# v by a transposing load, paired scores, re-laid first keys and a new order for the first eight tiles, in a fused attention and feed-forward kernel

## The chip, the cores and the metric

The kernel runs on one core of one Trainium2 chip. The metric is the time of one execution in device microseconds. TensorE is called PE here, VectorE DVE, ScalarE ACT, GpSimd POOL and SyncE SP, as in the profile; PEld is PE's loading of weights.

## The reference

```python
kv_pool = kv.reshape(B, H // r, r, W // r, r, C).mean(axis=(2, 4))   # r = 4
k = v = kv_pool.reshape(B, -1, C) @ w_sr                  # 4 x 768 x 128
s = (1 / sqrt(C)) * (q @ k.transpose(0, 2, 1))            # q: 4 x 12288 x 128
s = s - s.max(-1, keepdims=True)
a = exp(s)
a /= a.sum(-1, keepdims=True) + 1e-09
x = a @ v
x_prev = x shifted by one row along the sequence, zero at the start
xk = mu_k * x + (1 - mu_k) * x_prev
xr = mu_r * x + (1 - mu_r) * x_prev
k = maximum(xk @ w_k, 0)                                  # w_k: 128 x 1024
out = sigmoid(xr @ w_r) * ((k * k) @ w_v)                 # w_v: 1024 x 128
```

All inputs and the output are float32. `mu_r` and `w_r` are scaled up by 64 in the inputs, `mu_k` and `q` by 8.

## The kernel before

There are four batches of 24 tiles, 96 tiles of T = 512 rows of q. A tile has four sub-tiles of 128 rows. Products that must be more exact than one 16-bit pass are sums of three passes over a high and a low part of each operand.

**A tile.** `qf` is loaded, ACT rounds it to `qh`, POOL takes the rest `ql`. For each sub-tile s, `S{s}` writes 128 x 768 scores into PSUM: in chunks of 512 and 256 columns first the corrections `ql` x `ksb` and `qb` x `ksl`, both 16-bit, then `qh` x `ksh` in float32r, which the profile shows as f32. DVE takes the row maximum (`nm`), ACT the exponential (`ex`, tile `pe`) with its sum, DVE the reciprocal (`rc`), ACT the high half of the probabilities (`f1`) and DVE the low half (`f2`), both in tile `pp`. A transposing load on SP (`tt`, `pT`<-`pp`) turns them. `AV0` to `AV5` multiply `pT` with the rows of v, `v1` high and `v2` low, into `px`; ACT and DVE make `xk` and `xr` from it; POOL the low parts. `ha`/`hb` make the hidden layer (`ph`, four pieces f of 256 columns of w_k), `r`, `k2`, `kh`, `kl` square it and split it, `va`/`vb` multiply with w_v into `pv`, `z` is the gate.

**Keys and v of a batch.** For batch 0 `first_keys` loads the 16 members of each pooling window (`L_a`, `L_b`: pieces of 512 and 256 columns, from `kv0`) and PE adds them up through `wsr` in float32 (`pk`). For a later batch DVE sums twelve blocks of windows (`br`, `acc`<-`kvt`, one per tile from tile SUM_AT on), and PE multiplies the sum (`pk0`, `pk1`). ACT scales it to `ks`. `ksh`, `ksl` and `ksb` are its parts for the scores. For v, DVE scales `ks` (`ksv`), PE transposes it in six 128 x 128 pieces (`pt0`, `pt1`), and ACT and DVE take its high and low half out of PSUM. `dg` is a diagonal matrix that PE multiplies with ones to spread per-channel maxima over all partitions; it shares `pt1`'s PSUM tile, and `xt` reads the result. PSUM tile `x` exists once, for `px`, `pz`, `pk`, `pt` and `cs`; the large `big` tiles for `S` and `ph` exist three times.

**The weights** w_k, w_v, w_r come as float64 bit patterns and are taken apart by DVE, ACT and POOL (`we` to `wo`), with one matmul `cs` per part.

**Order.** Every step is a function in a heap, sorted by a number, and each engine runs its instructions in just that order. `ONCE` has the numbers of the once-only steps, `EARLY` those of the first eight tiles, `WHEN` those of all others (plus i x PERIOD, 19.3), `LATE` those of the last four, `PREP` those of a later batch's preparation (from PREP_AT tiles on). All DMAs are issued by SP, in the same order, and an issue can wait until an earlier DMA has landed or a buffer is free.

Of the kernel before, what the change touches and what calls it, by code (L numbers as in the profile page):

```python
# [11 lines left out]
F32 = mybir.dt.float32  # L12
# [59 lines left out]
def tile_kernel(ctx, tc, qT, kv0, kvw, w_sr, mu_k, mu_r, w_k, w_v, w_r, outT):  # L72
    nc = tc.nc
# [23 lines left out]
    wsr = const.tile([P, C], F32, name="wsr")  # L97
    nc.sync.dma_start(out=wsr, in_=w_sr)
# [8 lines left out]
    mu = const.tile([P, 2], F32, name="mu")  # L107
# [6 lines left out]
    for name, shape, dtype in (  # L114
# [8 lines left out]
        ("ksh", [P, K], F32R), ("ksl", [P, K], BF16), ("ksb", [P, K], BF16), ("v1", [P, NK, P], F16), ("v2", [P, NK, P], F16),  # L123
        ("s4", [P, 4], F32), ("uz", [P, 3], F32), ("sc", [P, 1], F32),
        ("ks", [P, K], F32), ("acc", [P, K], F32), ("dg", [P, 2, P], F32),
# [208 lines left out]
    def first_keys(ks, ksh, ksl, ksb):  # L334
        st = {"a": 0, "b": 0}
        for i in range(WIN // 2):
            home, row = FIRST["homes"][i]

            @once(f"L_a{i}")
            def _(i=i, home=home, row=row):  # L340
                if ("home", home) not in st:
                    if home < 2:
                        st["home", home] = take("pT", name="kva", shape=[P, 6, 512], dtype=F32)
                    else:
                        st["home", home] = take("kv", name="kva", shape=[P, 2, 512])
                st[f"a{i}"] = st["home", home][:, row:row + 2, :]
                sp.dma_start(out=st[f"a{i}"], in_=kv0[:, 2 * i:2 * i + 2, 0:512])
# [12 lines left out]
        for i in range(WIN // 4):  # L360
            @once(f"L_b{i}")
            def _(i=i):
                st[f"b{i}"] = take("kv", name="kvb", shape=[P, 4, K - 512])
                sp.dma_start(out=st[f"b{i}"], in_=kv0[:, 4 * i:4 * i + 4, 512:K])
# [95 lines left out]
    def batch_prep(b, i0, res):  # L460
# [12 lines left out]
        v1, v2, s4, uz, sc = (take(n) for n in ("v1", "v2", "s4", "uz", "sc"))  # L473
# [3 lines left out]
        res += [ksh, ksl, ksb, v1, v2, s4, uz, sc]  # L477
# [21 lines left out]
        @at("ksv")  # L499
        def _():  # L500
            st["ksv"] = take("acc", name="ksv")
            if FIRST["ksv"] == "A" and not later:
                act.activation(out=st["ksv"], in_=ks, func=AF.Copy, scale=ivs)
            else:
                dve.tensor_scalar_mul(st["ksv"], ks, ivs)

        for h, (j0, j1) in enumerate(((0, 4), (4, NK))):
            @at(f"pt{h}")
            def _(h=h, j0=j0, j1=j1):
                pt = st["pt", h] = take("x", name="pt", shape=[P, 4, P])  # L510
                for j in range(j0, j1):
                    pe.transpose(pt[:, j - j0, :], st["ksv"][:, j * P:(j + 1) * P], ident)
                if h:
                    pe.matmul(pt[:, 2:4, :], lhsT=ones, rhs=st["dg"], start=True, stop=True)

            @at(f"v1{h}")
            def _(h=h, j0=j0, j1=j1):
                act.copy(out=v1[:, j0:j1, :], in_=st["pt", h][:, 0:j1 - j0, :])

            @at(f"v2{h}")  # L520
            def _(h=h, j0=j0, j1=j1):
                dve.tensor_tensor(
                    out=v2[:, j0:j1, :], in0=st["pt", h][:, 0:j1 - j0, :], in1=v1[:, j0:j1, :],
                    op=ALU.subtract,
                )
# [19 lines left out]
    def plan_tile(i, b, t):  # L545
# [302 lines left out]
    for i, (b, t) in enumerate(seq):  # L848
# [13 lines left out]
SUM_AT = 5  # L862
PREP_AT = 18
# [323 lines left out]
```

## Time and profile before

| what | value |
|---|---|
| median of 3 runs (lowest to highest) | 1888.08 us (1887.74 to 1889.31) |
| the profiled execution | 1887.83 us |
| its span, first to last instruction | 1886.1 us |
| PE, DVE, ACT, POOL busy in the span | 99%, 94%, 90%, 61% |
| mean granted clock of PE | 0.999 |
| chain that ended last | PE 88%, DVE 9%, issue 2% |

The rows below come from the profiled execution. Times are us from the start of its span. A timeline's row gives start, length, engine, line, instruction, output <- input, shape and count; a bracket behind it is the idle time before it and what ended it. The recorded length of a matmul contains the time in which the next one already runs, so the pace of PE is read from starts, not from lengths. In this kernel almost all instructions have the line of a helper (L37); they are told apart by their tiles.

### The profile page before, as it was taken

The numbers are of one execution on the slowest core, as the hardware profiler recorded it, in microseconds if no ns is written. First come the engines' busy times: TensorE is split into PE (matmuls) and PEld (weight loads), VectorE is DVE, ScalarE is ACT, GpSimd is POOL, SyncE is SP. The second block draws the span as 40 slices with busy tenths as digits, with TensorE's granted clock in tenths as the row PEclk, the third lists the DMA queues.
The fourth block names the chain that finished last, engine by engine and source line by source line (L and its number), as shares of the span: only waits on it lengthen the run. The fifth ranks groups of instructions, "written<-read, shape, count | busy, mean of one in ns | idle before, by whom it ended". The sixth has DMA issues, their size and how long they took to land.

```text
span 1886.1 us, 26968 instructions
## 1 busy us (share of the span) xinstructions
PE 1864.4 (99%) x9089; PEld 908.7 (48%) x9089; DVE 1765.3 (94%) x2575; ACT 1705.0 (90%) x2441; POOL 1157.7 (61%) x784
## 2 busy tenths in 40 slices
PE   8899999999999999999999999999999999999999
PEld 5444444444444444444444444444444444444444
DVE  7999999999999999999899999999989899898998
ACT  5898998999999999899999999989999999999987
POOL 2465656665656666675657575757666666666555
PEclk9999999999999999999999999999999999999999
DMA  7757555465666665555667566645555555655462
GB/s 241 150 127 147 133 123 118 93 124 101 132 133 140 140 137 121 107 118 106 118 124 145 134 142 135 126 90 114 110 112 113 109 115 108 117 107 112 101 112 57
DMA packets 640524, 230.59 MB, mean 122 GB/s; under 512 B 606336, under 2 KB 608640, under 8 KB 640384
## 3 DMA queue, kind: packets, MB, share of 16 engines
q1 hardware_dynamic: 640384, 228.85, 58.5%
q8 instruction: 72, 1.18, 0.3%
q14 instruction: 68, 0.56, 0.1%
HBM read 52.63 MB, written 25.17 MB: 41 GB/s over the span
## 4 chain that ended last, share of the span: by engine, by line
PE 88%; DVE 9%; issue 2%; ACT 1%; DMA 1%; SPq 0%; DVEq 0%; ACTq 0%
PE ph L37 24%; PE pv L37 24%; PE px L37 18%; PE S L37 18%; PE pz L37 3%; DVE nm L37 2%; DVE pp L37 2%; PE pk L37 1%; DVE kl L37 1%; DVE kk L37 1%; DVE ph L37 1%; DMA kva<-kv 0%; DVE E L37 0%; DVE kh L37 0%; DVE xk L37 0%
## 5 line engine op out<-in xcount | busy, mean ns | idle before, releaser
L37 POOL TENSOR_TENSOR kl<-kk,kh 128x1024 bf16<-128x1024 f32 x288 | 683.4, 2373 | 57.8 <-DVE kh L37 16.7
L37 DVE TENSOR_REDUCE nm<-S 128x1 f32<-128x768 f32 x384 | 363.6, 948 | 81.6 <-PE S L37 81.3
L37 POOL TENSOR_TENSOR xrl<-xr,xrh 128x512 f16<-128x512 f32 x96 | 112.4, 1171 | 522.8 <-DVE xrh L37 514.2
L37 DVE SCALAR_TENSOR_TENSOR pp<-pe,rc,pp 128x768 f16<-128x768 f32 x384 | 419.9, 1111 | 8.7 <-ACT pp L37 8.5
L37 PE MATMUL px<-pT,v 128*128 128x512 f16 x1728 | 421.6, 380 | 1.6 <-DMA pT<-pp 1.3
L37 ACT ACTIVATE rr<-ph 128x1024 f32<-128x1024 f32 x384 | 389.8, 1016 | 32.8 <-PE ph L37 31.5
L37 ACT ACTIVATE pe<-S,nm 128x768 f32<-128x768 f32 x384 | 344.0, 896 | 69.7 <-DVE nm L37 67.9
L37 ACT ACTIVATE pp<-pe,rc 128x768 f16<-128x768 f32 x384 | 339.1, 930 | 42.9 <-ACT pe L37 36.4
L37 ACT ACTIVATE kh<-rr 128x1024 f16<-128x1024 f32 x288 | 303.3, 1054 | 0.9
L37 PE MATMUL ph<-xkh,wkl 128*128 128x512 f16 x768 | 292.3, 381 | 1.3 <-DVE kl L37 1.3
L37 PE MATMUL pv<-kh,wvl 128*128 128x512 f16 x768 | 292.0, 380 | 0.0
L37 PE MATMUL ph<-xkh,wkh 128*128 128x512 f16 x768 | 291.5, 379 | 0.0
L37 PE MATMUL pv<-kh,wvh 128*128 128x512 f16 x768 | 291.1, 379 | 0.0
L37 PEld LDWEIGHTS <-v 128*128 128x128 f16 x1728 | 168.8, 98 | 206.8 <-issue 3.8
L37 PE MATMUL S<-ksb,ql 128*128 128x512 bf16 (+1 forms) x768 | 252.1, 328 | 11.2 <-ACT pe L37 7.0
L37 DVE TENSOR_TENSOR kk<-ph,rr 128x1024 f32<-128x1024 f32 x192 | 233.2, 1215 | 2.6 <-ACT rr L37 2.6
L37 PEld LDWEIGHTS <-wkh 128*128 128x128 f16 x1536 | 150.4, 98 | 170.3 <-issue 1.2
L37 PE MATMUL S<-ksl,qh 128*128 128x512 bf16 (+1 forms) x768 | 229.4, 326 | 0.0
L37 PE MATMUL ph<-xkl,wkh 128*128 128x512 f16 x768 | 228.6, 380 | 0.0
L37 PE MATMUL S<-ksh,qh 128*128 128x512 f32 (+1 forms) x768 | 227.9, 378 | 0.0
L37 PE MATMUL pv<-kl,wvb 128*128 128x512 bf16 x768 | 226.7, 379 | 0.0
L37 POOL TENSOR_TENSOR xkl<-xk,xkh 128x512 f16<-128x512 f32 x96 | 144.1, 1501 | 97.9 <-DVE xkh L37 96.8
(120 smaller groups left out, 2448.5 us busy)
## 6 DMA issues: line engine op xcount, KB each, us to landing
qf<-qT SPq DMA_DIRECT2D x96, 256.0 KB, 3.5
outT<-o SPq DMA_DIRECT2D x96, 256.0 KB, 3.0
kvt<-kvw SPq DMA_DIRECT2D x36, 512.0 KB, 4.2
pT<-pp SPq DMA_TRANSPOSE x384, 3.8
kva<-kv SPq DMA_DIRECT2D x8, 512.0 KB, 9.6
kvb<-kv SPq DMA_DIRECT2D x4, 512.0 KB, 7.8
raw<-moe_w_k SPq DMA_DIRECT2D x2, 512.0 KB, 6.0
raw<-moe_w_v SPq DMA_DIRECT2D x2, 512.0 KB, 10.3
```

What stands on the lines that cost most here:

```text
L37: return self.tc.keep_in_program_order(op(*args, **kwargs))
```

## The change

- v's rows: ACT writes `ks` times `ivs` in fp16 (`vh`), DVE the rest (`vl`), into `vv`, and one transposing load on SP (`tv`) writes `vT`, which `AV` reads in place of `v1` and `v2`. `ksv`, the six transposes and the four copies go. `dg` is bf16 now and gets a PSUM tile of its own, by one matmul (`xm`).
- `mu_k` and `mu_r` come as two more columns of `w_sr` (`wm`); their two loads go.
- `kv0` lies in memory block by block, so that each partition's share of a block is 4 KB in one piece. It was 2 x 2 KB for `L_a` and 4 x 1 KB for `L_b`.
- SUM_AT and PREP_AT rise by 3, and `PREP` has new numbers.
- The scores of odd sub-tiles start with `qh` x `ksh` and end with the corrections; even ones as before.
- `EARLY` and `ONCE` have new numbers. `WHEN` and `LATE` stay.

```diff
-    wsr = const.tile([P, C], F32, name="wsr")
-    nc.sync.dma_start(out=wsr, in_=w_sr)
+    wm = const.tile([P, C + 2], F32, name="wm")
+    nc.sync.dma_start(out=wm, in_=wmu)
+    wsr, mu = wm[:, 0:C], wm[:, C:C + 2]
...
-            sp.dma_start(out=mu[:, i:i + 1], in_=src.rearrange("(p o) -> p o", o=1))
...
-                sp.dma_start(out=st[f"a{i}"], in_=kv0[:, 2 * i:2 * i + 2, 0:512])
+                sp.dma_start(out=st[f"a{i}"], in_=kv0[i].rearrange("p (w k) -> p w k", w=2))
...
-                sp.dma_start(out=st[f"b{i}"], in_=kv0[:, 4 * i:4 * i + 4, 512:K])
+                sp.dma_start(out=st[f"b{i}"], in_=kv0[WIN // 2 + i].rearrange("p (w k) -> p w k", w=4))
...
-        @at("ksv")
-        def _():
-            st["ksv"] = take("acc", name="ksv")
...
-                dve.tensor_scalar_mul(st["ksv"], ks, ivs)
...
-                    pe.transpose(pt[:, j - j0, :], st["ksv"][:, j * P:(j + 1) * P], ident)
-                if h:
-                    pe.matmul(pt[:, 2:4, :], lhsT=ones, rhs=st["dg"], start=True, stop=True)
...
-                act.copy(out=v1[:, j0:j1, :], in_=st["pt", h][:, 0:j1 - j0, :])
...
-                dve.tensor_tensor(
-                    out=v2[:, j0:j1, :], in0=st["pt", h][:, 0:j1 - j0, :], in1=v1[:, j0:j1, :],
-                    op=ALU.subtract,
-                )
+        @at("vh")
+        def _():
+            st["vv"] = take("vv")
+            act.activation(out=st["vv"][:, 0, :], in_=ks, func=AF.Copy, scale=ivs)
+
+        @at("vl")
+        def _():
+            dve.scalar_tensor_tensor(
+                out=st["vv"][:, 1, :], in0=ks, scalar=ivs, in1=st["vv"][:, 0, :],
+                op0=ALU.mult, op1=ALU.subtract,
+            )
+
+        @at("tv")
+        def _():
+            sp.dma_start_transpose(out=vT, in_=st["vv"].rearrange("p a k -> p (a k)"))
+
+        @at("xm")
+        def _():
+            st["xm"] = take("x", name="xm", shape=[P, 2, P])
+            pe.matmul(st["xm"], lhsT=ones_b, rhs=st["dg"], start=True, stop=True)
...
-                for c0, c1 in CHUNKS:
-                    o = S[:, c0:c1]
-                    pe.matmul(o, lhsT=ql, rhs=ksb[:, c0:c1], start=True, stop=False)
-                    pe.matmul(o, lhsT=qb, rhs=ksl[:, c0:c1], start=False, stop=False)
-                for c0, c1 in CHUNKS:
-                    pe.matmul(S[:, c0:c1], lhsT=qh, rhs=ksh[:, c0:c1], start=False, stop=True)
+                for main in ((False, True) if s % 2 == 0 else (True, False)):
+                    for c0, c1 in CHUNKS:
+                        o, end = S[:, c0:c1], s % 2
+                        if main:
+                            pe.matmul(o, lhsT=qh, rhs=ksh[:, c0:c1], start=bool(end), stop=not end)
+                        else:
+                            pe.matmul(o, lhsT=ql, rhs=ksb[:, c0:c1], start=not end, stop=False)
+                            pe.matmul(o, lhsT=qb, rhs=ksl[:, c0:c1], start=False, stop=bool(end))
...
-SUM_AT = 5
-PREP_AT = 18
+SUM_AT = 8
+PREP_AT = 21
...
-    "pk0": 5.759, "ks0": 6.167, "pk1": 9.402, "ks1": 11.701, "am": 15.804, "ex": 17.408,
...
+    "pk1": 9.683, "ks1": 10.495, "pk0": 10.786, "ks0": 12.243, "am": 12.806, "ksh": 14.072,
...
+    "ksl": 73.883, "ksb": 91.01, "vl": 92.312, "tv": 131.828,
```

The scores on PE (numbers behind a name tell buffers apart). In a steady tile the sub-tiles 0 and 1 stand next to each other, and 2 and 3. From the last correction of a pair's first one on, before:

```order
L37 MATMUL S_3827<-ksl_89,qh_3474 128x256
L37 MATMUL S_3827<-ksh_88,qh_3474 128x512
L37 MATMUL S_3827<-ksh_88,qh_3474 128x256
L37 LDWEIGHTS ql_3571
L37 MATMUL S_3839<-ksb_90,ql_3571 128x512
L37 LDWEIGHTS qh_3474
L37 MATMUL S_3839<-ksl_89,qh_3474 128x512
```

and now:

```order
L37 MATMUL S_4440<-ksl_88,qh_4094 128x256
L37 MATMUL S_4440<-ksh_87,qh_4094 128x512
L37 MATMUL S_4440<-ksh_87,qh_4094 128x256
L37 MATMUL S_4452<-ksh_87,qh_4094 128x512
L37 MATMUL S_4452<-ksh_87,qh_4094 128x256
L37 LDWEIGHTS ql_4186
L37 MATMUL S_4452<-ksb_89,ql_4186 128x512
L37 LDWEIGHTS qh_4094
L37 MATMUL S_4452<-ksl_88,qh_4094 128x512
```

The second sub-tile's `ksh` matmuls moved up to those of the first; a matmul in f32 has no row of its own for its weights here.

SP at the program's start: `wsr`/`wm` is w_sr, `raw` a half of w_k or w_v, `kva` and `kvb` blocks of the first keys. Before:

```order
L98 DMA wsr<-w_sr 128x128
L37 DMA raw<-moe_w_k 128x1024
L37 DMA kva<-kv 128x2x512
L37 DMA raw<-moe_w_k 128x1024
L37 DMA mu<-moe_mu_k 128x1
L37 DMA mu<-moe_mu_r 128x1
L37 DMA kva<-kv 128x2x512 x3
L37 DMA raw<-moe_w_v 128x1024
```

and now:

```order
L98 DMA wm<-wmu 128x130
L37 DMA raw<-moe_w_k 128x1024 x2
L37 DMA kva<-kv 128x1024 x4
L37 DMA raw<-moe_w_v 128x1024
L37 DMA kva<-kv 128x1024 x2
```

The two loads of `mu` are gone, and the second half of w_k moved ahead of the first block of keys.

DVE in the filling, at the first row maxima (`nm`) of tile 0; `pp` is `f2`, `v2` a subtraction for v, `acc` a sum for batch 1. Before, from the second `nm` on:

```order
L37 TENSOR_REDUCE nm_430<-S_399 128x1
L37 TENSOR_SCALAR dg_432<-ident_64,ex_96,mtop_84 128x128 x2
L37 TENSOR_REDUCE nm_435<-S_412 128x1
L37 TENSOR_SCALAR rc_444<-sm_437 128x2
L37 RECIPROCAL rc_444<-rc_444 128x2
L37 TENSOR_REDUCE nm_461<-S_452 128x1
L37 TENSOR_TENSOR v2_92<-pt_425,v1_91 128x512
L37 SCALAR_TENSOR_TENSOR pp_450<-pe_442,rc_444,pp_450 128x768
L37 SCALAR_TENSOR_TENSOR pp_459<-pe_438,rc_444,pp_459 128x768
L37 TENSOR_REDUCE nm_481<-S_468 128x1
L37 TENSOR_REDUCE acc_496<-kvt_382 128x64
```

and now:

```order
L37 TENSOR_SCALAR dg_394<-ident_64,ex_94,mtop_83 128x128 x2
L37 TENSOR_REDUCE nm_404<-S_381 128x1
L37 TENSOR_REDUCE nm_420<-S_397 128x1
L37 TENSOR_REDUCE nm_433<-S_406 128x1
L37 SCALAR_TENSOR_TENSOR vv_415<-ks_86,ivs_96,vv_415 128x768
L37 TENSOR_SCALAR rc_441<-sm_417 128x2
L37 RECIPROCAL rc_441<-rc_441 128x2
L37 TENSOR_REDUCE mx_wr_444<-cs_431 128x1
L37 TENSOR_REDUCE nm_446<-S_424 128x1
L37 SCALAR_TENSOR_TENSOR pp_448<-pe_436,rc_441,pp_448 128x768
L37 SCALAR_TENSOR_TENSOR pp_464<-pe_418,rc_441,pp_464 128x768
```

`dg` moved ahead of the first `nm`, the first sum left the stretch, and one subtraction for v stands where the first of two stood.

## Rows read from the trace of the kernel before

**Rows 1.** Windows: stretch, length, busy time per engine (count), clock, DMA share, GB/s.

```profile
7.50:10.00 2.50, 2.50 (x19) 1.87 (x18) 1.39 (x3) 1.42 (x3) 0.00 (x0) 1.00 0.64 204
...
12.50:15.00 2.50, 2.50 (x6) 1.08 (x7) 1.32 (x1) 1.15 (x2) 2.45 (x2) 1.00 1.04 400
...
34.20:64.40 30.20, 21.33 (x116) 12.43 (x115) 29.36 (x62) 24.46 (x46) 6.28 (x7) 1.00 0.77 162
...
820.00:880.00 60.00, 60.00 (x298) 29.26 (x296) 55.87 (x79) 56.02 (x80) 43.03 (x28) 1.00 0.56 110
```

**Rows 2.** Timeline of PE, one pair of scores: start, length, instruction, count.

```profile
699.82 0.38 PE L37 MATMUL ph<-xkh,wkl 128*128 128x512 f16 x1
...
703.92 0.38 PE L37 MATMUL S<-ksb,ql 128*128 128x512 bf16 x1
...
704.35 0.27 PE L37 MATMUL S<-ksb,ql 128*128 128x256 bf16 x1
...
704.46 0.27 PE L37 MATMUL S<-ksl,qh 128*128 128x256 bf16 x1
...
704.92 0.39 PE L37 MATMUL S<-ksb,ql 128*128 128x512 bf16 x1
...
705.93 0.39 PE L37 MATMUL ph<-xkh,wkl 128*128 128x512 f16 x1
```

**Rows 3.** Groups by form, the f32 weight loads: count, busy us, mean ns.

```profile
L37 PEld LDWEIGHTS S<-ksh,qh 128*128 128x128 f32 x768 | 116.0, 191 | 4.4
```

**Rows 4.** Timeline of PE, a batch change from 760.77 to 821.50.

```profile
760.77 0.38 PE L37 MATMUL S<-ksb,ql 128*128 128x512 bf16 x1
...
768.63 0.39 PE L37 MATMUL S<-ksb,ql 128*128 128x512 bf16 x1
...
769.65 0.59 PE L37 MATMUL pk<-acc,wsr 128*128 128x256 f32 x2
...
791.62 0.39 PE L37 MATMUL ph<-xkh,wkl 128*128 128x512 f16 x1 [0.45 <-DVE kl L37]
...
808.85 0.60 PE L37 MATMUL pt<-ident,ksv 128*128 128x128 f32 x4
...
809.28 0.38 PE L37 MATMUL pv<-kh,wvl 128*128 128x512 f16 x1
...
811.03 0.44 PE L37 MATMUL pt<-ident,ksv 128*128 128x128 f32 x2
...
811.74 0.38 PE L37 MATMUL ph<-xkh,wkl 128*128 128x512 f16 x1
...
821.50 0.38 PE L37 MATMUL S<-ksb,ql 128*128 128x512 bf16 x1
```

**Rows 5.** Timeline of PE, the start: first keys, first scores, first `ph`.

```profile
9.15 1.88 PE L37 MATMUL pk<-kva,wsr 128*128 128x512 f32 x4
...
12.34 5.42 PE L37 MATMUL pk<-kva,wsr 128*128 128x512 f32 x12 [1.31 <-DMA kva<-kv]
...
34.25 0.38 PE L37 MATMUL S<-ksb,ql 128*128 128x512 bf16 x1 [1.68 <-ACT ksb L37]
...
64.44 0.39 PE L37 MATMUL ph<-xkh,wkl 128*128 128x512 f16 x1
```

**Rows 6.** Timeline of DVE, the filling: first `nm`, first `xk`.

```profile
35.52 0.95 DVE L37 TENSOR_REDUCE nm<-S 128x1 f32<-128x768 f32 x1
...
62.54 0.75 DVE L37 SCALAR_TENSOR_TENSOR xk<-px,s,xek 128x512 f32<-128x512 f32 x1 [0.30 <-ACT xek L37]
```

**Rows 7.** Groups by form, what DVE does for sums and v.

```profile
L37 DVE TENSOR_REDUCE acc<-kvt 128x64 f32<-128x1024 f32 x36 | 43.5, 1210 | 0.0
...
L37 DVE TENSOR_TENSOR v<-pt,v 128x512 f16<-128x512 f32 x4 | 2.7, 672 | 0.0
```

**Rows 8.** Timelines of SP and ACT in the filling: transposing loads, ACT behind them.

```profile
42.58 8.43 SPq L37 DMA_TRANSPOSE pT<-pp  x4
...
60.42 0.93 ACT L37 ACTIVATE pp<-pe,rc 128x768 f16<-128x768 f32 x1 [1.94 <-DMA pT<-pp]
```

More of the change, by code (lines that the diff above doesn't have):

```diff
@@ L71, in tile_kernel @@
 @with_exitstack
-def tile_kernel(ctx, tc, qT, kv0, kvw, w_sr, mu_k, mu_r, w_k, w_v, w_r, outT):
+def tile_kernel(ctx, tc, qT, kv0, kvw, wmu, w_k, w_v, w_r, outT):
     nc = tc.nc
@@ L106, in tile_kernel @@
     wrh, wrl = (const.tile([P, P], F16, name=n) for n in ("wrh", "wrl"))
-    mu = const.tile([P, 2], F32, name="mu")
     mix = const.tile([P, 4], F32, name="mix")
@@ L122, in tile_kernel @@
         ("kl", [P, 2 * T], BF16), ("kv", [P, 1024], F32),
-        ("ksh", [P, K], F32R), ("ksl", [P, K], BF16), ("ksb", [P, K], BF16), ("v1", [P, NK, P], F16), ("v2", [P, NK, P], F16),
+        ("ksh", [P, K], F32R), ("ksl", [P, K], BF16), ("ksb", [P, K], BF16), ("vv", [P, 2, K], F16), ("vT", [P, 2 * NK, P], F16),
         ("s4", [P, 4], F32), ("uz", [P, 3], F32), ("sc", [P, 1], F32),
-        ("ks", [P, K], F32), ("acc", [P, K], F32), ("dg", [P, 2, P], F32),
+        ("ks", [P, K], F32), ("acc", [P, K], F32), ("dg", [P, 2, P], BF16),
     ):
@@ L156, in _ @@
             pe.matmul(pw, lhsT=ones_b, rhs=ones.bitcast(BF16), start=True, stop=True)
-    @once("L_mu")
-    def _():
-        for i, src in enumerate((mu_k, mu_r)):
-            sp.dma_start(out=mu[:, i:i + 1], in_=src.rearrange("(p o) -> p o", o=1))
     @once("mix")
@@ L472, in batch_prep @@
         (later_keys if later else first_keys)(*((b, i0, at) if later else ()), ks, ksh, ksl, ksb)
-        v1, v2, s4, uz, sc = (take(n) for n in ("v1", "v2", "s4", "uz", "sc"))
+        vT, s4, uz, sc = (take(n) for n in ("vT", "s4", "uz", "sc"))
         ex, exs, ivs = (one(n) for n in ("ex", "exs", "ivs"))
@@ L476, in batch_prep @@
         exi = one("exi", I32)
-        res += [ksh, ksl, ksb, v1, v2, s4, uz, sc]
+        res += [ksh, ksl, ksb, vT, s4, uz, sc]
         st = {}
@@ L497, in _ @@
                 )
-        @at("ksv")
+        @at("vh")
         def _():
-            st["ksv"] = take("acc", name="ksv")
-            if FIRST["ksv"] == "A" and not later:
-                act.activation(out=st["ksv"], in_=ks, func=AF.Copy, scale=ivs)
-            else:
-                dve.tensor_scalar_mul(st["ksv"], ks, ivs)
[L507 to L511, printed above, removed]
-                    pe.transpose(pt[:, j - j0, :], st["ksv"][:, j * P:(j + 1) * P], ident)
-                if h:
-                    pe.matmul(pt[:, 2:4, :], lhsT=ones, rhs=st["dg"], start=True, stop=True)
-            @at(f"v1{h}")
-            def _(h=h, j0=j0, j1=j1):
-                act.copy(out=v1[:, j0:j1, :], in_=st["pt", h][:, 0:j1 - j0, :])
-            @at(f"v2{h}")
-            def _(h=h, j0=j0, j1=j1):
-                dve.tensor_tensor(
-                    out=v2[:, j0:j1, :], in0=st["pt", h][:, 0:j1 - j0, :], in1=v1[:, j0:j1, :],
-                    op=ALU.subtract,
-                )
+            st["vv"] = take("vv")
[13 more added lines that the diff above has]
+            pe.matmul(st["xm"], lhsT=ones_b, rhs=st["dg"], start=True, stop=True)
         @at("xt")
         def _():
-            dve.tensor_reduce(out=xt, in_=st["pt", 1][:, 2:4, :], axis=AX.X, op=ALU.max)
+            dve.tensor_reduce(out=xt, in_=st["xm"], axis=AX.X, op=ALU.max)
         @at("sv")
@@ L653, in _ @@
             def _(j=j):
-                v1, v2 = bps[b][3:5]
+                vT = bps[b][3]
                 name = f"AV{j}"
@@ L657, in _ @@
                     st["px"] = take("x", name="px")
-                for m, (w, a) in enumerate(((v1, 1), (v2, 0), (v1, 0))):
+                for m, (c, a) in enumerate(((0, 1), (1, 0), (0, 0))):
                     pe.matmul(
-                        st["px"], lhsT=w[:, j, :], rhs=st["pT"][:, :, a * NK + j, :],
+                        st["px"], lhsT=vT[:, c * NK + j, :], rhs=st["pT"][:, :, a * NK + j, :],
                         start=(name == av_first and m == 0), stop=(name == av_last and m == 2),
@@ L673, in _ @@
                     out=shifted(x)[:, 1:T + 1], in_=st["px"], func=AF.Copy,
-                    scale=bps[b][5][:, k + 1:k + 2],
+                    scale=bps[b][4][:, k + 1:k + 2],
                 )
@@ L687, in _ @@
                 dve.scalar_tensor_tensor(
-                    out=new(f"x{x}"), in0=st["px"], scalar=bps[b][5][:, k:k + 1],
+                    out=new(f"x{x}"), in0=st["px"], scalar=bps[b][4][:, k:k + 1],
                     in1=st[f"xe{x}"][:, 0:T], op0=ALU.mult, op1=ALU.add,
@@ L714, in _ @@
             def _():
-                act.activation(out=new("th"), in_=st["pz"], func=AF.Tanh, scale=bps[b][6][:, 1:2])
+                act.activation(out=new("th"), in_=st["pz"], func=AF.Tanh, scale=bps[b][5][:, 1:2])
             @at("T1")
@@ L723, in _ @@
             def _():
-                act.activation(out=new("th"), in_=st["pz"], func=AF.Abs, scale=bps[b][6][:, 0:1])
+                act.activation(out=new("th"), in_=st["pz"], func=AF.Abs, scale=bps[b][5][:, 0:1])
             @at("th")
@@ L732, in _ @@
             def _():
-                act.activation(out=new("E"), in_=st["pz"], func=AF.Relu, scale=bps[b][6][:, 2:3])
+                act.activation(out=new("E"), in_=st["pz"], func=AF.Relu, scale=bps[b][5][:, 2:3])
             @at("E")
@@ L740, in _ @@
             def _():
-                act.activation(out=new("E"), in_=st["pz"], func=AF.Exp, scale=bps[b][6][:, 0:1])
+                act.activation(out=new("E"), in_=st["pz"], func=AF.Exp, scale=bps[b][5][:, 0:1])
             @at("E1")
             def _():
-                dve.tensor_scalar(st["E"], st["E"], 1.0, bps[b][7], op0=ALU.min, op1=ALU.mult)
+                dve.tensor_scalar(st["E"], st["E"], 1.0, bps[b][6], op0=ALU.min, op1=ALU.mult)
         @at("g")
@@ L830, in _ @@
                 dve.scalar_tensor_tensor(
-                    out=new("o"), in0=st["pv"], scalar=bps[b][7], in1=st["E"],
+                    out=new("o"), in0=st["pv"], scalar=bps[b][6], in1=st["E"],
                     op0=ALU.mult, op1=ALU.mult,
@@ L1139, in build @@
     tile_kernel(
-        tc, ins["qT"], ins["kv0"], ins["kvw"], ins["w_sr"], ins["moe_mu_k"], ins["moe_mu_r"],
+        tc, ins["qT"], ins["kv0"], ins["kvw"], ins["wmu"],
         *(words(ins[n]) for n in ("moe_w_k", "moe_w_v", "moe_w_r")), out,
@@ L1157, in layout, with chunks @@
     kvw = kv.reshape(B, H // r, r, W // r, r, C)
+    first = np.ascontiguousarray(kvw[0].transpose(4, 1, 3, 0, 2)).reshape(C, r * r, K)
+    def chunks(rows, n):
+        return rows.reshape(C, -1, n, rows.shape[2]).transpose(1, 0, 2, 3).reshape(-1, C, n * rows.shape[2])
     return {
         "qT": np.ascontiguousarray(q.transpose(0, 2, 1)),
-        "kv0": np.ascontiguousarray(kvw[0].transpose(4, 1, 3, 0, 2)).reshape(C, r * r, K),
+        "kv0": np.concatenate([chunks(first[:, :, :512], 2), chunks(first[:, :, 512:], 4)]),
         "kvw": np.ascontiguousarray(kvw[1:].transpose(0, 5, 1, 3, 2, 4)).reshape(B - 1, C, K, r * r),
-        "w_sr": np.ascontiguousarray(w_sr),
-        "moe_mu_k": np.ascontiguousarray(moe_mu_k),
-        "moe_mu_r": np.ascontiguousarray(moe_mu_r),
+        "wmu": np.concatenate([w_sr, moe_mu_k[:, None], moe_mu_r[:, None]], axis=1),
         "moe_w_k": bits(moe_w_k),
```

8 lines of the change are left out of this document (4 added, 4 removed), and 286 rows, old and new, of tables (EARLY, ONCE, PREP).

## The prediction

> **What bounds the kernel now.** I read the windows first. In a steady stretch, 820 to 880 us, PE is busy for the whole 60.00 us, DVE for 55.87, ACT for 56.02 and POOL for 43.03, and DMA's share is 0.56 [rows 1]. So a nanosecond off PE's own work there comes off the time, and work that moves between the other engines does not, as long as DVE keeps some of its 4.1 us of idle time. Second, the timeline of PE for one tile. The 19 matmuls of 512 columns from 699.82 to 703.92 take 4.10 us, 0.2158 each; one of 256 columns takes 0.11 (704.35 to 704.46), which I count as 0.109 [rows 2]. A tile has 69 of 512 columns outside the scores, 14.89 us, and four groups of scores of three long and three short ones, 0.974 each. That is 18.79. A tile takes 18.95: from 703.92 to 760.77 lie three [rows 2, 4]. The missing 0.166 us is 0.041 per group of scores, and the starts show where it sits: 1.00 from 703.92 to 704.92 and 1.01 to 705.93 instead of 0.974 [rows 2]. A group goes from 16-bit operands to `ksh` in f32 and back, once each, and that change is what costs.
>
> Third, a batch change: from 760.77 to 821.50 are 60.73 us, three tiles are 56.85, so the preparation of a batch costs PE 3.88 us [rows 4], three times. Last, the start. PE's first keys begin at 9.15 behind the warm-up, stop once for 1.31 us on a load of `kva`, and the first scores begin at 34.25; the first `ph` is at 64.44 [rows 5]. In between PE is busy 21.33 of 30.20 us, ACT 24.46, and DVE 29.36 [rows 1]: DVE sets the pace of the filling. After it PE is nearly full, so what the filling saves stays saved.
>
> The profiled execution took 1887.83 us (span 1886.1), 0.25 below the median of 1888.08; I sum against 1887.83. A measurement can tell about 0.2%, 3.8 us, from no change.
>
> **Paired scores.** Odd sub-tiles now take `ksh` first. In the order, 384 separate runs of `ksh` matmuls become 207, so 177 pairs lose one change into f32 and one back: 177 x 0.041 = 7.3 us, less what the new neighbourhood costs. That is a load of other f32 weights behind a `ksh` matmul of only 256 columns (0.109). The load is recorded at 191 ns [rows 3], but two places bound what of it shows. In today's groups it already stands behind a 256-column matmul, and all that the group loses, both changes included, is 0.041. And before `pk` f32 weights are loaded behind a `ksh` matmul of 256 columns: that group takes 1.02 (768.63 to 769.65) where one followed by 16-bit weights takes 1.01 [rows 2, 4]. So between 0 and 0.02; I take 0.005, since 0.01 is the rounding of these rows. 177 x 0.036 = **-6.4 us**, between -3.7 and -7.3. Nothing else is due earlier or later: a pair ends where it ended, its `nm` with it.
>
> The Trainium skill says, in "TensorE: Matmul & The Clock Gate", section "LDWEIGHTS (loading the stationary operand)", that a load takes its columns divided by 1.2 GHz, so 107 ns for 128. By that an estimate would hide the load wholly behind 0.109, and the term would be -7.3. The recorded 191 ns disagrees with it in length; what no row of before shows is a `ksh` load behind another `ksh` matmul of 256 columns.
>
> **v by a transposing load.** Per batch PE drops six transposes and two passes over `dg`: 808.85 to 809.28 and 811.03 to 811.74 [rows 4], 0.43 + 0.71 = 1.14 us, and gets one 16-bit matmul of 256 columns, 0.11. That is 1.03 on the path. The two f32 `pk` stay, 0.43 (as 2 x 0.215 at 769.65) and twice that, 1.29. Of the 3.88 us 1.45 are waits, the longest at 791.62, where PE idles 0.45 on DVE's `kl` [rows 4]. DVE loses `ksv` and two subtractions for one subtraction of 768 columns; its own row of 512 is 672 ns [rows 7], so about 1.1 stands against 0.6 + 1.1, and the rest is spread over seven tiles instead of three. I let 0.35 of the 1.45 go. Three batches: 3 x 1.4 = **-4.2 us**. The bounds are new waits of 0.5 per batch, -1.6, and no waits at all, -7.4. In the first batch the transposes lie in the filling, where PE waits anyway: nothing. ACT trades two copies for one instruction, nothing in 820 to 880 [rows 1]. The load `tv` queues on SP ahead of `tt` loads, but is placed 39 us after its `vl` and 15 us before its first reader; SP needed 8.43 us for four such loads [rows 8], 2.1 each. So it hides; the cover is gone only if v were late by some 10 us.
>
> **Sums three tiles later.** As many sums, 36 of 1.21 us [rows 7], in other tiles; a steady tile is 18.95 with them, so DVE's idle time covers them there. In the filling there is no idle time, so the three that leave it count (below). The last part of the new keys, `ksb`, still stands 28 us of plan ahead of the first scores that read it: nothing. Without that cover each sum would cost up to 1.13.
>
> **Start.** `mu` rides with `w_sr` and its two small loads go; around them, 7.5 to 10 us, DMA's share is 0.64 at 204 GB/s against 1.04 and 400 later [rows 1]. Both halves of `w_k` now come ahead of the first keys, but four blocks of keys follow them without a gap, in 4 KB pieces. From 9.15 PE works on the first keys almost in a row, and the one hole is the 1.31 us that end at 12.34 [rows 5]. So the start can give 1.3 at most, and it could lose as much if the first block came later behind 0.5 MB more (1.3 us at 400 GB/s); I take **-1.3 us**, since the hole follows the slow stretch that goes.
>
> **First eight tiles anew.** PE does 15 groups of scores before the first `ph`, before and after. From the first `nm` at 35.52 to the first `xk` at 62.54 [rows 6] DVE is full. An instruction there costs its row less 0.08, since the next begins before it ends. DVE loses one sum (1.13), v's subtractions (0.59 + 0.33), half of `wvl` and a piece of `wrl`'s chain that go behind (0.66 + 0.26 + 0.18), and `dg`, now ahead of the first `nm` (0.50): 3.65. It gains `vl` (1.03) and `mx_wr` (0.19): **-2.4 us**. Two more sums leave before tile 7 is done, and what went behind comes back, so the gain holds. Start and filling together: -3.7. The ends are -7 (the three sums whole, the clock's dip behind the filling gone too) and +1 (the second rival).
>
> **Sum.** 1887.8 - 6.4 - 4.2 - 3.7 = **1873.5 us**.
>
> **Rivals.** (1) The f32 load shows. If a second sub-tile's weights can't be loaded behind the first one's last `ksh` matmul, each pair waits 191 - 109 = 82 ns, and if the 0.041 belongs to every group and not to the change of type, nothing comes back: 177 x 0.082 = +14.5 and 1887.8 + 14.5 - 4.2 - 3.7 = 1894.4, slower. It decides from 68 ns per pair. For it speaks the 191 [rows 3]; against it that groups lose only 0.041 with that very load behind that very length [rows 2], and `pk` [rows 4]. (2) The filling hangs on the transposing loads and not on DVE. ACT stood 1.94 us behind them at 60.42, and four took 8.43 [rows 8]; `tv` is one more ahead of all of them, +2.1 in place of -2.4: 1878.0. Against it: two loads of sums leave the same stretch, and DMA's share is 0.77 [rows 1]. (3) The new order of the first tiles is better than its DVE sum, because waits of PE after 64 us go as well, and a batch loses its waits: -7 and -7.4, 1867.0.
>
> **How the numbers follow.** Forecast 60%, second rival (with smaller forms of it, and batches that keep all waits) 23%, third 11%, first 6%. The range reaches from the third rival to past the second, with the pair term at its weak end (+2.7) and half of the batch's missing: 1867 to 1882. Faster by over 0.2% is below 1884.1: all but the first rival and 0.03 of the second, 0.91. Within 0.2%: that 0.03 and 0.01 of the first rival, should its wait be half as long. Slower: the other 0.05.
>
> **What would show it.** Right: a steady tile at 18.88 in place of 18.95, both groups of a pair together near 1.98 in place of 2.01; a batch change of 2.5 us in place of 3.9; first scores near 33 and first `ph` near 60.7. Wrong: a pair longer than 2.02 (first rival), first `ph` at 64 or later (second), PE waiting for `vT` at the first tile of a batch, or the clock low in the stretch after the filling for longer than before.

## The result, and the profile of the changed kernel

The changed kernel takes 1872.89 us (median of 4 runs, 1871.34 to 1873.66); the kernel before took 1888.14 beside it. The ratio is 0.9917, with a 95% interval of 0.9900 to 0.9934. The forecast was 1873.5, but two of its terms are off by more than 3 us, in opposite directions. The profiled execution took 1873.66 us, span 1871.9; it is the slowest of the four.

To see where the time went, I laid the two traces side by side by the start of the first row maximum (`nm`) of each tile on DVE:

| first `nm` of tile | before | after | difference | what lies between |
|---|---|---|---|---|
| 0 | 35.52 | 34.70 | -0.82 | start |
| 13 | 265.32 | 260.73 | -4.59 | filling and first tiles |
| 25 | 496.66 | 489.26 | -7.40 | batch change 1 |
| 36 | 705.12 | 697.37 | -7.75 | steady tiles |
| 49 | 955.37 | 944.77 | -10.60 | batch change 2 |
| 60 | 1163.89 | 1153.00 | -10.89 | steady tiles |
| 73 | 1414.18 | 1400.46 | -13.72 | batch change 3 |
| 89 | 1717.38 | 1703.18 | -14.20 | steady tiles |

The steady stretches lose 0.35, 0.29 and 0.48 in 11, 11 and 16 tiles: 0.029 a tile, 2.8 in 96 tiles. With that taken off (0.35 or 0.38 each), a batch change gives 2.46, 2.47 and 2.45, together 7.4. Start and first tiles give 4.59 - 0.38 = 4.2. That is 14.4 of the spans' 14.2. The 4.2 moves with the execution: in the kernels v_back and old_prep below, whose program is the same up to the first batch change, the first `nm` of tile 13 comes at 259.56 and 258.39 in place of 260.73.

The windows of after: stretch, length, busy time per engine (count), clock, DMA share, GB/s.

```profile
7.50:10.00 2.50, 2.50 (x20) 1.96 (x19) 2.43 (x7) 1.22 (x2) 0.68 (x1) 1.00 1.02 419
32.60:62.60 30.00, 22.28 (x108) 11.72 (x109) 28.43 (x57) 24.74 (x45) 9.34 (x11) 0.94 0.86 158
690.00:750.00 60.00, 59.74 (x291) 29.52 (x295) 58.65 (x85) 55.84 (x81) 37.58 (x25) 1.00 0.64 138
```

PE is as full in a steady stretch as before, and DMA's share at 7.5 to 10 us rose from 0.64 to 1.02 [rows 1]. The timeline of PE in the start and the filling:

```profile
9.26 5.32 PE L37 MATMUL pk<-kva,wm 128*128 128x512 f32 x12
...
32.67 0.38 PE L37 MATMUL S<-ksb,ql 128*128 128x512 bf16 x1 [1.73 <-ACT ksb L37]
...
51.30 5.08 PE L37 MATMUL px<-pT,vT 128*128 128x512 f16 x15 [1.83 <-DMA pT<-pp]
...
62.63 0.39 PE L37 MATMUL ph<-xkh,wkl 128*128 128x512 f16 x1 [1.17 <-DVE xkh L37]
```

The hole of 1.31 us is gone and the first scores come 1.58 us earlier, at 32.67 [rows 5]. The first `ph` comes only 1.81 earlier. DVE in the filling:

```profile
33.47 1.31 DVE L37 TENSOR_SCALAR dg<-ident,ex,mtop 128x128 bf16<-128x128 f32 x1
34.70 2.67 DVE L37 TENSOR_REDUCE nm<-S 128x1 f32<-128x768 f32 x3
...
57.43 0.96 DVE L37 TENSOR_REDUCE nm<-S 128x1 f32<-128x768 f32 x1 [1.15 <-PE S L37]
58.30 1.97 DVE L37 SCALAR_TENSOR_TENSOR pp<-pe,rc,pp 128x768 f16<-128x768 f32 x1
...
61.06 0.73 DVE L37 SCALAR_TENSOR_TENSOR xk<-px,s,xek 128x512 f32<-128x512 f32 x1
```

From the first `nm` to `xk` there are 26.36 us, before 27.02 [rows 6]. Three things took the rest of the gain. The second `dg`, which now stands ahead of the first `nm`, takes 1.31 where each takes 0.33 to 0.35 in later batches; so the first `nm` begins 2.03 behind the first scores, before 1.27. One `pp` took 1.97 where others take 1.0. And DVE waited 1.15 for scores. The two long instructions are in the traces of all eleven kernels with the new order of the first tiles (1.30 to 1.32 and 1.96 to 2.01), and in none of the three with the old one. Both stand beside POOL's `ql`, but no run shows why they are long.

The scores that DVE waited for were late because `px` ran at half clock. In the windows of 52 to 56 us the granted clock (ahead of DMA's share) is 0.65 in after (first row), and 1.00 in v_back, where it had fallen earlier, to 0.67 at 44 to 48 us. In old_prep it did not fall, and the same 15 `px` took 3.40 in place of 5.08 (last row).

```profile
52.00:56.00 4.00, 4.00 (x13) 1.52 (x12) 3.97 (x7) 4.00 (x8) 2.40 (x3) 0.65 1.20 197
```

```profile
52.00:56.00 4.00, 4.00 (x22) 1.99 (x20) 3.96 (x7) 4.00 (x8) 2.39 (x3) 1.00 1.08 198
```

```profile
50.16 3.40 PE L37 MATMUL px<-pT,vT 128*128 128x512 f16 x15 [1.80 <-DMA pT<-pp]
```

Steady tiles on PE, then batch change 2:

```profile
696.18 0.70 PE L37 MATMUL S<-ksb,ql 128*128 128x512 bf16 x2
...
734.02 0.70 PE L37 MATMUL S<-ksb,ql 128*128 128x512 bf16 x2
...
809.70 0.38 PE L37 MATMUL S<-ksb,ql 128*128 128x512 bf16 x1
...
818.26 0.59 PE L37 MATMUL pk<-acc,wm 128*128 128x256 f32 x2
...
857.42 0.27 PE L37 MATMUL xm<-dg,ones_b 128*128 128x256 bf16 x1
...
867.89 0.38 PE L37 MATMUL S<-ksb,ql 128*128 128x512 bf16 x1
```

Two tiles take 37.84, so one takes 18.92 (18.95 before). From 809.70 to 867.89 are 58.19 us, and three tiles are 56.76: a batch change costs 1.43 us where it cost 3.88 [rows 4]. That is what PE's own work makes, 1.29 of `pk` and 0.11 of `xm`; no wait is left. A pair of scores in after:

```profile
715.10 0.38 PE L37 MATMUL S<-ksb,ql 128*128 128x512 bf16 x1
...
715.64 0.27 PE L37 MATMUL S<-ksl,qh 128*128 128x256 bf16 x1
715.67 0.94 PE L37 MATMUL S<-ksh,qh 128*128 128x512 f32 x4
716.45 0.39 PE L37 MATMUL S<-ksb,ql 128*128 128x512 bf16 x1
...
717.11 0.38 PE L37 MATMUL ph<-xkh,wkl 128*128 128x512 f16 x1
```

It takes 2.01, as before [rows 2]. Rounding hides the gain, so I averaged the starts of all complete pairs without a wait, up to the second matmul behind them (the first two steps behind f32 are long): 2.246 us before (170 pairs), 2.232 after (127). So a pair saves 15 ns by its own starts and 16 by the length of the tiles (2.8 us in 177 pairs).

### The profile page after: what moved, and what is told of

Read it like the earlier page. It is cut to its first block, busy times and chain, and to the rows that moved or that the text cites. A ratio compares the mean times of both kernels' runs of the same rounds, so it can differ in the third digit from the quotient of the medians.

```text
span 1871.9 us, 26944 instructions
## 1 busy us (share of the span) xinstructions
PE 1847.1 (99%) x8915; PEld 921.1 (49%) x9061; DVE 1764.2 (94%) x2567; ACT 1703.6 (91%) x2437; POOL 1161.4 (62%) x784
## 4 chain that ended last, share of the span: by engine, by line
PE 95%; DVE 3%; ACT 1%; issue 1%; DMA 0%; DVEq 0%; ACTq 0%
PE ph L37 26%; PE pv L37 25%; PE px L37 19%; PE S L37 19%; PE pz L37 4%; PE pk L37 1%; DVE nm L37 1%; DVE pp L37 1%; PE pw L37 0%; ACT rr L37 0%; DMA pT<-pp 0%; DVE xr L37 0%; DVE xk L37 0%; DVE kh L37 0%; ACT kh L37 0%
## 5 line engine op out<-in xcount | busy, mean ns | idle before, releaser
L37 PE MATMUL px<-pT,vT 128*128 128x512 f16 x1728 | 421.7, 380 | 1.9 <-DMA pT<-pp 1.8
L37 PEld LDWEIGHTS <-vT 128*128 128x128 f16 x1728 | 169.3, 98 | 206.4 <-issue 4.6
L37 PE MATMUL S<-ksb,ql 128*128 128x256 bf16 (+1 forms) x762 | 249.6, 328 | 8.1 <-ACT pe L37 3.9
L37 PE MATMUL S<-ksl,qh 128*128 128x512 bf16 (+1 forms) x721 | 214.2, 322 | 0.4
L37 PE MATMUL pv<-kl,wvb 128*128 128x512 bf16 x675 | 206.9, 379 | 0.4
L37 PE MATMUL S<-ksh,qh 128*128 128x512 f32 (+1 forms) x768 | 186.0, 361 | 1.7 <-ACT pe L37 1.7
```

The source lines that it names most:

```text
L37: return self.tc.keep_in_program_order(op(*args, **kwargs))
```

## The experiments

Each ran beside the kernel before, whose median was 1888.1 to 1888.5 in all three groups; the changed kernel's 1872.89 is what they are set against. It was not run again beside them, and its four runs spread over 2.3 us, so a difference of less than that rests on the traces.

**unpaired**: the scores' loop of before, all else as in after.

```diff
-                for main in ((False, True) if s % 2 == 0 else (True, False)):
...
+                for c0, c1 in CHUNKS:
+                    o = S[:, c0:c1]
...
+                for c0, c1 in CHUNKS:
+                    pe.matmul(S[:, c0:c1], lhsT=qh, rhs=ksh[:, c0:c1], start=False, stop=True)
```

> The changed kernel with every sub-tile's scores in the order of before (corrections first, ksh last). Theory A, from the two traces: in a pair the second sub-tile's ksh matmuls, behind the first one's last ksh matmul of 256 columns, take 24 ns longer than their columns, and what a pair saves is 15 ns, not 36. Then 177 x 0.015 = +2.6, 1875.5 us. Theory B, the prediction's term: 177 x 0.036 = +6.4, 1879.3 us. A steady tile should be back at 18.95.

Measured: 1876.65 us (1875.49 to 1877.78), +3.8. By the traces the loss grows evenly to 4.1 us, 23 ns per pair; a pair, counted as above, takes 2.256. Between the theories, nearer A. But that is 10 ns more than a pair of before, whose matmuls stand in the same order.

**before_paired**: the kernel before, with the new loop as its only change.

```diff
-                for c0, c1 in CHUNKS:
...
+                for main in ((False, True) if s % 2 == 0 else (True, False)):
...
```

> The kernel before with paired scores as its only change. Theory A: each pair loses one change of type and back, 24 ns, as between the changed kernel with and without pairing: 177 x 0.024 = -4.2, 1883.9 us. Theory B: 15 ns, as between the pairs of the two kernels: -2.6, 1885.5 us. Theory C, the prediction's 36 ns: -6.4, 1881.7 us. A steady tile goes to 18.90, 18.92 or 18.88.

Measured: 1887.54 (1885.83 to 1889.24), ratio 0.9993 (0.9984 to 1.0002), -1.0. The gain between tile 8 and tile 95 is 1.5 us, 9 ns per pair. C and A fall. B's -2.6 is within the interval, which ends at -3.0, but high by the trace. Pairing alone can hardly be told from no change.

**short_first**: even sub-tiles take the corrections of the 256 columns first.

```diff
-                    for c0, c1 in CHUNKS:
+                    for c0, c1 in (CHUNKS if main or s % 2 else CHUNKS[::-1]):
```

> The changed kernel; in even sub-tiles the corrections of the 256 columns come first and those of the 512 columns last, so that the first ksh weights in f32 are loaded behind a matmul of 512 columns. Theory A: the step from 16-bit into f32 costs 19 ns because the load, recorded at 191 ns, stands behind only 109 ns. Then 192 sub-tiles x 19 ns = -3.6, 1869.3 us, and a pair takes 1.997 in place of 2.016. Theory B: the change of type itself costs that, whatever stands before it: 0, 1872.9 us.

Measured: 1872.65 (1871.77 to 1873.35), -0.2; a pair 2.231 in place of 2.232. Theory A falls: a matmul of 512 columns ahead of the load, in place of 256, changes nothing that can be seen.

**thirds**: a pair's first `ksh` matmul of 512 columns split in two.

```diff
-                    for c0, c1 in CHUNKS:
+                    for c0, c1 in (((0, 256), (256, 512), (512, K)) if main and s % 2 == 0 else CHUNKS):
...
```

> The changed kernel; in even sub-tiles the ksh matmul of 512 columns is split into two of 256, so that a pair has five f32 matmuls in place of four. Theory A: every f32 matmul takes some 10 ns beyond its columns and each change between 16-bit and f32 and back 24 ns (a group of two f32 matmuls loses 45 without pairing, a pair's four lose 66): a pair goes from 2.016 to 2.016 + 0.010 + 0.002 = 2.028, and the whole by 192 x 0.012 = +2.3. Theory B: the f32 matmuls cost only their columns, and the pair's loss sits at the junction of two sub-tiles: 2.018, +0.4.

Measured: 1873.46, one execution. In its trace a pair takes 2.237, 6 ns more than in after, and a tile 0.011 more: between A's 12 and B's 2, a little nearer B. From the last correction ahead of `ksh` to the first one behind it, a pair in thirds:

```profile
714.85 0.27 PE L37 MATMUL S<-ksl,qh 128*128 128x256 bf16 x1
714.88 0.94 PE L37 MATMUL S<-ksh,qh 128*128 128x256 f32 x5
715.66 0.39 PE L37 MATMUL S<-ksb,ql 128*128 128x512 bf16 x1
```

0.81 with five matmuls, 0.81 with four in after (715.64 to 716.45). By the means, one more matmul with its load costs 6 ns, and 2 of these are columns (twice 117 against 232, see below): some 4 ns at most are a price of its own. The single starts inside show what costs more: from one f32 matmul to the next, on the mean, 117 ns for 256 columns and 232 for 512, where 16-bit takes 109 and 216. So f32 columns are 7% slower, 0.455 ns against 0.422. Of the 41 ns that a group lost, 8 + 16 = 24 are that, and stay when it is paired; some 17 are the change, and a pair saves one of these. That fits the 15 and 16 ns between the two kernels, not the 9 of before_paired and the 23 of unpaired. The order is not all that sets a pair's pace: in after, the first pair of a tile takes 2.241 us in the first and third batch (20 pairs) and 2.228 in the second and fourth (23), with the f32 matmuls alone differing; kv0_rows, below, has 2.237 and 2.230. The batches use two buffers of the keys by turns, so the place of the operands is a rival for differences of this size. No run tests it.

**v_back**: later batches make v as before, at the numbers of before, three tiles later.

```diff
+            @at("ksv")
...
+                    pe.transpose(pt[:, j - j0, :], st["ksv"][:, j * P:(j + 1) * P], ident)
...
+    "pk0": 5.759, "ks0": 6.167, "pk1": 9.402, "ks1": 11.701, "am": 15.804, "ex": 17.408,
...
```

> The changed kernel; in the three later batches v is made as before (ksv, six transposes, four copies, dg in f32 in the same PSUM tile), with the preparation numbers of before, still three tiles later. Theory A: a batch change goes from 1.4 us over the steady tiles back to 3.9, because PE again waits for DVE: 3 x 2.45 = +7.4, 1880.3 us. Theory B, the prediction's: 1.4 per batch, +4.2, 1877.1 us. Theory C: only PE's own work of 1.03 comes back, because the waits went through the three tiles' shift: +3.1, 1876.0 us.

Measured: 1880.03 (1879.07 to 1881.21), +7.1; 2.56, 2.53 and 2.57 us per batch in the trace. Theory A. The batch change, first and last row, takes 60.73, to the hundredth what it took in before [rows 4]:

```profile
811.08 0.70 PE L37 MATMUL S<-ksb,ql 128*128 128x512 bf16 x2
...
871.81 0.38 PE L37 MATMUL S<-ksb,ql 128*128 128x512 bf16 x1
```

**old_prep**: v by the transposing load, but at the numbers of before.

```diff
-    "pk1": 9.683, "ks1": 10.495, "pk0": 10.786, "ks0": 12.243, "am": 12.806, "ksh": 14.072,
...
+PREP = {'pk0': 5.759, 'ks0': 6.167, 'pk1': 9.402, 'ks1': 11.701, 'am': 15.804, 'ex': 17.408, 'dg': 25.684, 'vh': 33.342, 'vl': 48.635, 'xm': 49.56, 'xt': 49.96, 'tv': 50.044, 'sv': 51.348, 'ksh': 54.09, 'ksb': 54.093, 'uz': 54.476, 'ksl': 70.41}
```

> The changed kernel; in the three later batches v comes by the transposing load as now, but every step of the preparation that both kernels have stands at its number of before, and the new ones at the places of the ones that they replace (vh at ksv, vl and tv at the two subtractions, xm at the second set of transposes), within three tiles again. Theory A: the waits went because DVE and PE have less to do at a batch change: 0 to +1, 1872.9 to 1873.9 us. Theory B: they went because the steps are spread over seven tiles: 3 x 1.45 = +4.3, 1877.2 us.

Measured: 1881.18 (1878.93 to 1881.40), +8.3; 2.54, 2.53 and 2.56 per batch. Worse than B: although PE has 1.03 us less to do, the batch change is as long as with the transposes. PE and DVE there:

```profile
809.90 0.70 PE L37 MATMUL S<-ksb,ql 128*128 128x512 bf16 x2
...
840.77 0.39 PE L37 MATMUL ph<-xkh,wkl 128*128 128x512 f16 x1 [0.47 <-DVE kl L37]
...
862.42 1.45 PE L37 MATMUL px<-pT,vT 128*128 128x512 f16 x6 [1.16 <-DVE xt L37]
...
870.62 0.38 PE L37 MATMUL S<-ksb,ql 128*128 128x512 bf16 x1
```

```profile
859.44 1.00 DVE L37 SCALAR_TENSOR_TENSOR vv<-ks,ivs,vv 128x768 f16<-128x768 f32 x1
...
861.96 0.42 DVE L37 TENSOR_REDUCE xt<-xm 128x2 f32<-128x256 f32 x1
```

`xm` started at 859.70, but `xt` stands behind `vl` and three others in DVE's order and ends at 862.4; `px` needs the same PSUM tile and waits 1.16 for it. What PE no longer does, it now waits, with `vl` at this place.

**v_back_spread**: transposes, at spread numbers (`ksv` 35, `pt1` 48.5, `pt0` 67.8, the rest as in after).

```diff
+            @at("ksv")
...
+                    pe.transpose(pt[:, j - j0, :], st["ksv"][:, j * P:(j + 1) * P], ident)
```

> The changed kernel; in the three later batches v is made by transposes on PE as before, but at numbers spread as in the changed kernel: pk, ks, ksh, ksl, ksb, dg, xt, sv, uz at the changed kernel's numbers, ksv at 35, the second set of transposes with dg at xm's 48.5, the first set one tile later at 67.8. Theory A: the spread takes the waits away by itself and PE's extra work stays on the path: a batch change of 1.4 + 1.03 = 2.4 us, 3 x 1.03 = +3.1, 1876.0 us. Theory B: the transposes make PE wait for DVE wherever they stand: 3.9 per batch again, +7.4, 1880.3 us.

Measured: 1877.86 (1877.65 to 1878.38), +5.0; 1.87 per batch, that is the 1.03 of work and 0.84 of new waits, of which one row is:

```profile
881.06 1.46 PE L37 MATMUL px<-pT,vT 128*128 128x512 f16 x6 [0.72 <-DVE vT L37]
```

Between the theories. The four kernels make a table of what a batch change costs PE over its tiles, from 1.43 plus the loss:

| | numbers of before | spread numbers |
|---|---|---|
| transposes | 4.0 | 3.3 |
| transposing load | 4.0 | 1.4 |

Neither the load nor the numbers give the gain: the load alone gives nothing, the numbers alone 0.7, both 2.5. This holds for the places tried: in the two mixed kernels the steps that have no number in the other one were put in by hand.

**mu_apart**: two loads for `mu` again, behind the first block of keys.

```diff
+            sp.dma_start(out=mu[:, i:i + 1], in_=src.rearrange("(p o) -> p o", o=1))
```

> The changed kernel with mu_k and mu_r loaded by two loads of their own again, behind the first block of keys. Theory A, the prediction's: these two small loads hold the queue, and the hole of 1.3 us before the fifth key matmul comes back: +1.3, 1874.2 us, first scores near 34.0. Theory B: the order of the loads (both halves of w_k first) or the 4 KB blocks made the hole go: 0, 1872.9 us.

Measured: 1875.88 (1874.63 to 1877.20), +3.0. Theory A, with more than twice its size. The first scores start at 35.32; the issues on SP, the DMAs (KB each, us to landing), the window and PE:

```profile
2.60 0.43 SPq L37 DMA_DIRECT2D mu<-moe_mu_k  x1
```

```profile
mu<-moe_mu_k SPq DMA_DIRECT2D x1, 0.5 KB, 5.8
```

```profile
7.50:10.00 2.50, 2.41 (x12) 1.14 (x9) 0.37 (x5) 0.00 (x0) 0.00 (x0) 1.00 0.80 277
```

```profile
11.19 3.70 PE L37 MATMUL pk<-kva,wsr 128*128 128x512 f32 x8 [0.86 <-DMA kva<-kv]
```

Half a KB takes 5.8 us to land, the second block of keys lands at 11.14 where it landed at 9.63 in after, and PE waits for it again.

**kv0_rows**: the first keys in memory as before.

```diff
-                sp.dma_start(out=st[f"a{i}"], in_=kv0[i].rearrange("p (w k) -> p w k", w=2))
+                sp.dma_start(out=st[f"a{i}"], in_=kv0[:, 2 * i:2 * i + 2, 0:512])
...
```

> The changed kernel with the first keys in memory as before, in pieces of 2 KB and 1 KB a partition in place of 4 KB. Theory A: the queue moved 400 GB/s with 2 KB pieces in the kernel before, so the blocks cost nothing: 0, 1872.9 us. Theory B: the smaller pieces, of 1 KB above all, are slower, and the first scores come later by what twelve loads lose, 0.1 each or more: +1.2 or more, 1874.1 us.

Measured: 1872.62 (1872.39 to 1873.29), -0.3: theory A. The first four blocks land 1.33 us apart, in after 1.28, but PE waits for none of them in either, so the 4 KB blocks give nothing to the time.

**old_first**: the numbers of before for the once-only steps and the first eight tiles.

```diff
-    "L_wk0": -43.319, "L_wk1": -30.923, "L_a1": -19.667, "warm": -6.626, "mix": 37.092,
...
+ONCE = {'L_wk0': -51.169, 'warm': -6.626, 'we_wk0': -2.2, 'wf_wk0': 10.361, 'wi_wk0': 24.085,
...
```

> The changed kernel with the numbers of before for the once-only steps and for the first eight tiles (vh and vl at the places of the first pair of copies, tv behind vl, xm at the second copy, no loads of mu). Theory A: the new numbers themselves give about half of what the start and the first tiles gain, since DVE and PE wait less: +2 to +4, 1875 to 1877 us. Theory B: the gain comes from the work that left these tiles (sums, copies for v, two loads) in whatever order: 0 to +1, 1873 to 1874 us.

Measured: 1876.88 (1876.83 to 1878.22), +4.0: theory A, at its end. Its first `nm` is 1.14 earlier than in after, its `xk` of tile 11 is 2.7 later. The key loads are issued in the order of before again, without those of `mu`, and PE has no hole in its first keys: the order of the two halves of w_k gives nothing.

**sums_one**: the sums one tile earlier, so that one stands in the filling.

```diff
-SUM_AT = 8
+SUM_AT = 7
```

> The changed kernel with the sums of each batch one tile earlier (7 in place of 8), the preparation where it is. In the first batch this brings one sum back into the filling, behind the second row maximum of tile 0 or so, its load behind those of the first keys. Theory A, the prediction's: DVE is full there, and a sum costs 1.13: +1.1, 1874.0 us. Theory B: DVE's waits in the filling cover it: 0 to +0.3, 1873.0 us.

Measured: 1874.47 (1874.35 to 1875.60), +1.6: theory A, a little more. By the first `nm` of each tile, nothing changes by more than 0.2 from tile 4 on; there it is 0.7 to 0.8 behind after and some 1.8 behind kv0_rows.

**sums_early**: sums and preparation three tiles earlier. This run missed its question.

```diff
-SUM_AT = 8
-PREP_AT = 21
+SUM_AT = 5
+PREP_AT = 18
```

> The changed kernel with the sums and the preparation of a batch three tiles earlier again (5 and 18). Theory A: DVE is full up to about tile 13, so the three sums that come back into tiles 5 to 7 and the ones that were already there cost their whole length: 3 x 1.13 = +3.4, 1876.3 us, and it shows in the first 250 us. Theory B: the sums fit into waits of DVE even there: 0 to +0.5, 1873.4 us. Batches 2 and 3 should not change in either.

Measured: 1881.57 (1881.00 to 1881.82), +8.7, but 6.1 of it stand already before the first `nm`, and the rest before the first `xk`. The new numbers place the first keys late, so the load of the first sum now stands ahead of some of them on SP:

```profile
7.35 0.33 SPq L37 DMA_DIRECT2D kvt<-kvw  x1
...
9.91 0.43 SPq L37 DMA_DIRECT2D kva<-kv  x1
...
20.69 0.33 SPq L37 DMA_DIRECT2D kvb<-kv  x1
```

What it does show: from tile 3 to tile 13 the difference stays at 7.9, so sums in those tiles cost nothing.

## Why the prediction came out, point by point

**Paired scores, -6.4 forecast, some -2.8 found**, beyond the weak bound of -3.7. The step that failed is "that change is what costs": the 41 ns were put down to the change between 16-bit and f32 as a whole. 24 of them are f32 columns at 0.455 ns, which pairing can't remove (thirds, short_first). The junction of two sub-tiles, which I sized at 5 ns, is hardly more than such columns: 117 ns go there as inside a sub-tile of thirds. The Trainium skill's rule in "TensorE: Matmul & The Clock Gate", section "LDWEIGHTS (loading the stationary operand)", is that a load takes its columns divided by 1.2 GHz, 107 ns for 128, which would hide behind 109. The traces agree with it in the effect, at most some 4 ns per load (thirds), and not in the length, since 191 ns are recorded [rows 3]. The 7.3 us that I drew from it were wrong with my own term, since that rule says nothing of f32 columns. The first rival (1894.4) is out.

**v by a transposing load, -4.2 forecast, -7.4 found**, the strong bound. PE's work was sized rightly, 1.03 and 1.29 that stays. The step that failed is the 0.35 of 1.45 that I let go: all 1.45 went. And the working added the parts up, where each needs the other, at the places tried: with the old numbers the 1.03 turn into a wait for `xt` (old_prep), with the transposes the spread turns into a wait for the subtraction (v_back_spread). `tv` hides, as forecast: in after it landed 5.5 us behind its issue in batch change 2, 4.0 in the median of four, and PE waited for `vT` nowhere.

**Sums three tiles later**: nothing in steady tiles, as forecast; one in the filling costs 1.6 in the median (sums_one), forecast 1.13; the clock's share in that is not told apart.

**Start, -1.3 forecast, -1.58 found at the first scores**, near 33 as said. It is the least that an execution shows: the first scores come 23.4 us behind the first key matmul in after, v_back and old_prep alike, and that one starts at 9.26, 8.60 and 8.08. In before and before_paired, where PE waits for keys, it starts at 9.15 and 8.15 and the scores come at 34.25 and 34.24. The two small loads are the cause, by more than I gave them (mu_apart, first `nm` 2.65 later); the 4 KB blocks and the order of the w_k halves do nothing (kv0_rows, old_first).

**First eight tiles, -2.4 forecast up to the first `ph`, -0.2 found in the profiled execution.** DVE's list of instructions was right. Two steps failed. `dg` was taken as 0.50 gained because it left the stretch, but DVE has no idle time ahead of the first `nm` either, and now holds it up. And every instruction was given its length of before, where one `dg` and one `pp` are 1.0 longer each. The rest is the clock. From the first scores to the first `ph` there are 30.19 us in before and 29.96 in after, and 28.75 in old_prep, the same program with the clock up throughout: some 1.2 us are the clock's, and 1.0 of the forecast is missing without it. That old_prep's first `ph` comes at 60.31, where 60.7 was forecast, it owes to its early start. Between the first `ph` and tile 13 another 2.4 us went, which I had as the third rival: the waits behind 64 us and the dip of the clock there (0.60 at 64 to 68 us in before), which lies ahead of the first `ph` in after. So start and first tiles gave 4.2, forecast 3.7. Their parts don't add up either: undone one at a time, `mu`, the numbers and one sum cost 3.0 + 4.0 + 1.6. That may be because the new numbers were made for the other parts; and in each of these three traces the clock stood at half two to three times as long as in after, which is in the price.

The errors of the pair term (+3.6) and of the batch term (-3.2) cancel, and that is luck: the time came out to 0.6 us, the mechanism of the scores did not. The second rival is out, since the first `ph` came earlier; the third came true by half.

## What to carry to other kernels

When a small loss has several possible owners (the change of type, the load, the columns), put the steps from start to start beside each other before giving all of it to one; three numbers inside a group would have told. Taking work off the busiest engine can come back as a wait, if the steps behind it on the other engines stay where they were; price the two together. A step that moves ahead of a stretch is not gone, if the engine is full there too. A load of a few bytes in a queue of large ones costs what it delays, not what it carries.

## What the runs showed of the hardware beyond that

- f32 matmuls passed 117 ns per 256 columns and 232 per 512 on the mean, 16-bit ones 109 and 216. By batch and pair the 232 goes from 229 to 237 in after, the 216 stays.
- A load of 0.5 KB took 5.8 us to land where 512 KB blocks beside it took 8.9.
- Two kernels with the same order of matmuls differ in the pace of a pair by 10 ns (before 2.246, unpaired 2.256), and two batches of one kernel by 13. No run tells why; it stays open.
- With the same program up to there, the granted clock fell to its lower level (half, 1.2 GHz) at 51 to 55 us in after, at 43 to 47 in v_back and not at all in old_prep, and the first `ph` came at 62.6, 61.5 and 60.3. Of these 2.3 us 1.1 stood already at the first scores (32.67 and 31.56).
